# Four block products at once: the small matrix M computed from 64x64 tiles of the tensor engine

## The chip, the cores and the metric

The kernel runs on one core of a Trainium2 chip. The metric is the device time of one execution in microseconds (us). Every time quoted as a median comes from executions without the profiler; each profile is of one further execution, and its span (first to last instruction) is a little shorter than the device time of the same run: 260.0 us of span against 261.42 us for the kernel before. All profiles that an argument rests on are of fast runs; two runs of one experiment, and its profile, fell in a slower state, and that is said there. Some runs of the kernel before did too (five among those below: 266.08, 267.37, 266.89, 266.29 and 266.42 us); they count in its medians, but not in the ratios.

Engines are named as in the profile: PE is the tensor engine (TensorE), PEld its weight loads, DVE VectorE, ACT ScalarE, POOL GpSimd, SP SyncE. "SPq" is SyncE's sequencer issuing a transfer. The kernel's PSUM tensor `ps`, where the matmuls write, is laid out as eight banks of 512 columns, used singly or as four pairs. The granted clock is TensorE's clock in the profile, as a share of full speed. In the timelines a w2 tile is ten matmuls (five of 512 columns, five of 128) for 128 tokens, a w3 group is five 512-column matmuls whose result ACT copies out of PSUM as `h2T`, and an a-tile is the ten matmuls of attention for 128 tokens.

## The reference, cut to what matters

```python
# A: linear attention, 32 heads of 20 columns; S = 2048 tokens, D = 640
pq, pk = phi(q), phi(k)                            # phi = elu + 1
kv  = einsum("bhsd,bhse->bhde", pk, v)             # one 20x20 matrix per head
num = einsum("bhqd,bhde->bhqe", pq, kv)
o   = num / den
a   = o @ wo
# B: LayerNorm, w1, gelu, token shifts, w2, residual, LayerNorm, w3, gelu, w4
out = g * a + (1 - g) * b
```

The kernel never forms `o`. The 32 head matrices and `wo` are contracted into one 640x640 matrix M first, and attention for a tile of 128 tokens is then one product with the normalised queries, `pqnT`:

M = blockdiag(kv) · wo,  a-tile = (pq / den) · M.

`blockdiag(kv)` is cut into blocks of whole heads. `GT` is x^T·phi(k), so a block of kv comes from the value weights and `GT`; its off-diagonal heads are masked away on the way into `Lt`, which is the weight operand of the product with `wo`. M lies in SBUF as `M_sb`, five slots of 128 rows.

## The kernel before

Before the change a block is six heads, 120 columns: five blocks of 120, and one of 40 for the last two heads. Each block gets its own product of one 512-column and one 128-column matmul. Blocks of 120 leave rows 120 to 127 of each slot of `M_sb` free; the 40 rows of the last block go there. They are first written to `Mt` and then moved by five small transfers of eight rows.

```python
def kvt_group(h):                                   # kv blocks; 30 small matmuls over h = 0, 1
    ...
    for q_, r in enumerate(range(4) if h == 0 else range(4, 6)):
        n = min(R6, D - R6 * r)                     # R6 = 120
        for k in range(KD):                         # KD = 5
            mms.append((ps[:, b, R6 * q_:R6 * q_ + n], wvf[:, D * k + R6 * r:D * k + R6 * r + 128],
                        GT[:, k, R6 * r:R6 * r + n], ...))
...
def m_group(r):                                     # one block of M, recorded six times
    n = min(R6, D - R6 * r)
    kr = R6 if r < 5 else 128
    b = pair()
    mm_group(ps[:, b, 0:512], [(Lt[0:kr, r, :], wo_aug[0:kr, r, 0:512])])
    mm_group(ps[:, b + 1, 0:128], [(Lt[0:kr, r, :], wo_aug[0:kr, r, 512:D])])
    src = psf[0:n, 512 * b:512 * b + D]
    dst = M_sb[0:n, r, :] if r < 5 else Mt[0:n, :]
    activation(dst, src, ACTF.Copy)                 # ACT writes only rows 0 to 119 of M_sb

def m_tail():                                       # rows 120 to 127 of every slot
    for j in range(KD):
        sch.dma("sp", M_sb[R6:128, j, :], Mt[8 * j:8 * j + 8, :], "mt", group_total=KD)
...
for n, r in enumerate((5, 0, 1, 2, 3, 4)):          # the block that feeds Mt comes first
    IT.add("KVF", ("m", r), 0.0, lambda r=r: m_group(r),
           deps=[(("lt", 1), 1.0), (("w3", (1 + 3 * n) // KFF, (1 + 3 * n) % KFF), 0.0)])
IT.add("MT", ("mt",), 0.0, m_tail, deps=[(("m", 5), 1.5), (("t1", NT - 1), 0.0)])
...
def qt_tile(t):                                     # pqnT by transposing transfers, also on SyncE
    sch.dma("sp", pqnT[:, :, 128 * t:128 * (t + 1)], pq_tok[:, t, :], ..., transpose=True)

def a_tile(t):                                      # the first use of M
    ...
    mm_group(ps[:, b, 0:512], [(pqnT[:, j, tok], M_sb[:, j, 0:512]) for j in range(KD)])
    mm_group(ps[:, b + 1, 0:128], [(pqnT[:, j, tok], M_sb[:, j, 512:D]) for j in range(KD)])
```

## Time and profile before

Three runs before the prediction: 261.96, 266.08 and 263.4 us, median 263.4.

| what | value | read from |
|---|---|---|
| span | 260.0 us, granted clock 1.00 | cores view |
| PE busy | 254.7 us, 98% | page, part 1 |
| chain that ended last | 97% PE | page, part 4 |
| one M block, from its first matmul to the next ordinary one | 0.27 to 0.28 us in five of the six; behind the other one a matmul's record is missing | PE timeline |
| row moves into M | 5 issues in 3.49 us, from 115.97 | SP timeline |
| first use of M | 139.42 us, no wait | PE timeline |

The page of the kernel before, parts 1 and 4, is:

```profile
PE 254.7 (98%) x1671; PEld 135.9 (52%) x1703; DVE 148.9 (57%) x266; ACT 106.9 (41%) x215; POOL 96.8 (37%) x151
...
PE 97%; issue 1%; DVE 1%; POOL 0%; POOLq 0%
```

PE is the bottleneck nearly everywhere. A change helps only by taking time from PE, and hurts as soon as it makes PE wait.

The PE timeline of the kernel before follows. Here and in every timeline below the columns are: start in us, us from the first start to the last end, engine, source line, operation, output and inputs, their shapes, number of instructions, and in brackets the idle time before the group and what ended it.

```profile
92.34 1.52 PE L600 MATMUL ps<-w,hsT 128*128 128x512 bf16 x10
...
126.17 0.44 PE L600 MATMUL ps<-wo_aug,Lt 120*128 120x512 bf16 x2
126.45 1.24 PE L600 MATMUL ps<-xnT,w 128*128 128x512 bf16 x5
...
139.42 1.52 PE L600 MATMUL ps<-M_sb,pqnT 128*128 128x512 bf16 x10
```

The first line is w2 tile 4, after which the changed kernel does its first M products. An M block takes the slot from 126.17 to 126.45, since a matmul's recorded duration overlaps the next one's start. The last line is the first use of M. The distance from 92.34 to 139.42, 47.08 us, holds everything that the change does to M. I call it the **M stretch** and compare it in every run: it leaves out the start of the kernel, whose length varies between runs.

SyncE's issues in the kernel before, from the SP timeline:

```profile
115.97 3.49 SPq L285 DMA_DIRECT2D M_sb<-Mt  x5
119.51 6.66 SPq L281 DMA_TRANSPOSE xnT<-xn  x4
126.21 7.88 SPq L281 DMA_TRANSPOSE pqnT<-pq_tok  x6
```

The row moves are over by 119.5, and the first pqnT transpose is issued at 126.21, some 13 us before its use.

### The profile page before, as it was taken

To read this page: it belongs to the slowest core of one execution; us is meant where nothing else is said; L and a number is where in the kernel's file an instruction comes from. 1 tells how busy PE (TensorE), PEld (TensorE's weight loads), DVE (VectorE), ACT (ScalarE), POOL (GpSimd) and SP (SyncE) were. 2 spreads that over 40 slices of the span, in tenths; PEclk is the share of its full clock that TensorE was granted. 3 is DMA by queue.
4 is the path that set the end of the run, shared out by engine and by line. 5 is a ranking of instruction groups with operands and counts; after the bars stand their busy time and mean duration, and the time that the engine had idled before them with its cause. 6 is when DMAs were issued, how large, how long until landed. Compare 5 with 4: busy or idle time off the path is not lost.

```text
span 260.0 us, 4263 instructions
## 1 busy us (share of the span) xinstructions
PE 254.7 (98%) x1671; PEld 135.9 (52%) x1703; DVE 148.9 (57%) x266; ACT 106.9 (41%) x215; POOL 96.8 (37%) x151
## 2 busy tenths in 40 slices
PE   8999999999999999999999999999999999999996
PEld 4555555555555454555444545554455544455553
DVE  1597877899903799979994407992033410143333
ACT  1496777741355757674874240005500045100000
POOL 5013995859874017865854202230011100021001
PEclk9999999999999999999999999999999999999999
DMA  6855989642566894355565700232000020000311
GB/s 199 255 103 143 211 149 158 194 87 23 105 126 103 275 377 94 76 101 58 107 124 109 125 0 0 45 85 74 3 0 0 3 101 0 3 0 0 103 50 50
DMA packets 50691, 24.82 MB, mean 95 GB/s; under 512 B 42052, under 2 KB 49261, under 8 KB 50672
## 3 DMA queue, kind: packets, MB, share of 16 engines
q1 hardware_dynamic: 49280, 21.15, 35.8%
q0 software_dynamic: 1152, 3.28, 5.2%
q8 instruction: 13, 0.21, 0.3%
q10 hardware_dynamic: 240, 0.13, 0.2%
q14 instruction: 6, 0.05, 0.1%
HBM read 12.05 MB, written 2.62 MB: 56 GB/s over the span
## 4 chain that ended last, share of the span: by engine, by line
PE 97%; issue 1%; DVE 1%; POOL 0%; POOLq 0%
PE ps L600 61%; PE ps L1106 21%; PE ps L781 8%; PE ps L857 2%; PE ps L830 1%; PE ps L1020 1%; PE ps L1088 1%; DVE x_tok L639 1%; PE ps L858 1%; PE ps L611 1%; PE ps L934 1%; PE ps L1085 0%; POOL xn L659 0%; POOLq L1249 0%
## 5 line engine op out<-in xcount | busy, mean ns | idle before, releaser
L600 PE MATMUL ps<-xnT,w 128*128 128x512 bf16 x349 | 80.7, 379 | 0.5
L1106 PE MATMUL ps<-w,h2T 128*128 128x128 bf16 (+1 forms) x409 | 57.9, 298 | 0.7 <-issue 0.5
L656 ACT ACTIVATE h2T<-ps 128x512 bf16<-128x512 f32 x52 | 30.5, 600 | 65.6 <-PE ps L600 65.5
L600 PEld LDWEIGHTS ps<-xnT,w 128*128 128x128 bf16 x360 | 33.9, 98 | 36.9 <-issue 0.4
L639 DVE SCALAR_TENSOR_TENSOR x_tok<-ps,stg,abx 128x512 bf16<-128x512 f32 (+1 forms) x32 | 17.2, 551 | 61.6 <-PE ps L1106 61.6
L622 POOL TENSOR_SCALAR abx<-x_tok,stg 128x640 f32<-128x640 bf16 x16 | 14.8, 923 | 100.6 <-DVE x_tok L639 95.1
L1106 PEld LDWEIGHTS ps<-w,h2T 128*128 128x128 bf16 x416 | 32.4, 98 | 25.6 <-issue 1.1
L622 POOL TENSOR_SCALAR xn<-x_tok,st 128x640 bf16<-128x640 bf16 x32 | 36.8, 1155 | 15.4 <-DMA xnT<-xn 14.9
L656 ACT ACTIVATE Er<-ps 128x640 bf16<-128x640 f32 x32 | 22.4, 704 | 17.4 <-PE ps L600 8.5
L655 ACT ACTIVATE junk<-x_tok 128x640 bf16<-128x640 bf16 x32 | 23.6, 737 | 4.9 <-DVE x_tok L637 4.4
L656 ACT ACTIVATE hsT<-ps 128x512 bf16<-128x512 f32 (+1 forms) x32 | 18.9, 593 | 15.1 <-PE ps L600 12.7
L600 PE MATMUL ps<-w,hsT 128*128 128x512 bf16 (+1 forms) x159 | 23.8, 298 | 0.1
L600 PE MATMUL ps<-M_sb,pqnT 128*128 128x128 bf16 (+1 forms) x156 | 23.5, 297 | 0.3
L781 PE MATMUL ps<-pk_tok,x_tok 128*128 128x128 bf16 (+1 forms) x156 | 23.3, 297 | 0.2
L639 DVE SCALAR_TENSOR_TENSOR abx<-ps,stg,abx 128x640 f32<-128x640 f32 x16 | 14.1, 884 | 15.3 <-PE ps L600 15.3
L600 PE MATMUL ps<-wkg,xT 128*128 128x512 bf16 (+1 forms) x147 | 22.3, 298 | 0.2
L600 PEld LDWEIGHTS ps<-w,hsT 128*128 128x128 bf16 x160 | 13.3, 98 | 12.3
L600 PEld LDWEIGHTS ps<-M_sb,pqnT 128*128 128x128 bf16 x160 | 13.1, 98 | 10.4
L600 PE MATMUL ps<-wq,xT 128*128 128x512 bf16 (+1 forms) x119 | 18.2, 298 | 0.1
L622 DVE TENSOR_SCALAR Er<-Er 128x640 bf16<-128x640 bf16 x32 | 12.0, 376 | 9.1 <-ACT Er L656 8.8
L637 DVE SCALAR_TENSOR_TENSOR x_tok<-ps,x_tok 128x640 bf16<-128x640 f32 x16 | 13.1, 821 | 6.9 <-PE ps L600 6.0
L600 PEld LDWEIGHTS ps<-wkg,xT 128*128 128x128 bf16 x150 | 12.2, 97 | 9.0
(71 smaller groups left out, 230.0 us busy)
## 6 DMA issues: line engine op xcount, KB each, us to landing
w<-in_B_w_dram SPq DMA_DIRECT2D x1, 2160.0 KB, 8.2
w<-in_B_w_dram SPq DMA_DIRECT2D x1, 2080.0 KB, 13.7
x_tok<-in_A_x_dram SPq DMA_DIRECT2D x3, 640.0 KB, 5.7
out_dram<-x_tok SPq DMA_DIRECT2D x3, 640.0 KB, 3.5
w<-in_B_w_dram POOLq DMA_DIRECT2D x8, 160.0 KB, 4.8
wq<-in_A_wqkv_dram SPq DMA_DIRECT2D x5, 160.0 KB, 3.8
wkg<-in_A_wqkv_dram SPq DMA_DIRECT2D x5, 160.0 KB, 3.9
wv<-in_A_wqkv_dram POOLq DMA_DIRECT2D x1, 800.0 KB, 6.2
```

The source lines that it names most:

```text
L600: ins = e.matmul(out_ap, l, r, start=(i == 0), stop=(i == n - 1))
L611: ins = e.transpose(o, s_, ident[:])
L622: return engf(lambda e: e.tensor_scalar(out_ap, in_ap, s1, s2, op0, op1), rd, [out_ap], cost=cost)
L637: return dve(lambda e: e.scalar_tensor_tensor(out_ap, in0, scalar, in1, op0, op1, accum_out=accum), rd, [out_ap, accum], cost=cost + 70.0)
L639: return dve(lambda e: e.scalar_tensor_tensor(out_ap, in0, scalar, in1, op0, op1), rd, [out_ap], cost=cost)
L655: return act(lambda e: e.activation(out_ap, in_ap, func, bias=bias, scale=scale, accum_out=accum), rd, wr, cost=cost)
L656: return act(lambda e: e.activation(out_ap, in_ap, func, bias=bias, scale=scale), rd, wr, cost=cost)
L781: ins = e.matmul(o, l, r, start=(t0 + q_ == 0), stop=(t0 + q_ == NT - 1))
L830: ins = e.matmul(ps[:, b, 0:n], xn[:, 0, 0:128], xn[:, 0, 0:128].unsqueeze(1).to_broadcast([128, n // 128, 128]), start=True, stop=True)
L857: e.matmul(ps[:, b, 0:512], l, w[:, k, 0:512], start=(k == 0), stop=(k == KD - 1))
L858: return e.matmul(ps[:, b + 1, 0:n2], l, w[:, k, 512:512 + n2], start=(k == 0), stop=(k == KD - 1))
L1106: ins = e.matmul(o, l, r, start=False, stop=(i == KFF - 1), skip_group_check=(n0 > 0))
```

## The change

The intent: the six block products cost six passes through PE's array, one after the other, and most of each product meets zeros, since only the heads' own 20x20 matrices are kept. With blocks of 60 columns (three heads), the array can be addressed as four 64x64 tiles, and up to four block products run at once. Eleven blocks are then three passes instead of six: one of three products (the last of the eleven blocks has 40 columns), recorded after w2 tile 4 (`m_last`), and two of four (`m_first`), recorded after the eighth w3 group. I call each visit to 64x64 tiles an *excursion*.

For this the kernel holds kv blocks at partitions 0 and 64: ACT copies the value weights into pairs of 60-column blocks (`wv2`, 25 copies). It also takes six PSUM banks at once for `m_first`, where blocks from the two halves of the array are given different banks. And the layout of M changes: free rows are now 60 to 63 and 124 to 127 of each slot, so ten row moves of four rows replace five of eight. The evictions of `m_first` are copies over all 128 partitions, which overwrite the free rows, so the row moves have to follow `m_first`.

```diff
-R6 = 120
+B3 = 60
+    wv2 = ra.alias("wv2", [128, KD, 6, 128], BF16, ...)        # value weights in pairs of blocks
+    def wv_blocks(k):                                           # 5 ACT copies for each k, 25 in all
+        ...
+    def kvt_group(h):   # still 30 matmuls; weights from wv2, up to 160 columns
...
-    def m_group(r):
-        ...             # as above
+    def m_step(jobs, tails):
+        def fn(e):
+            ins = None
+            for step in jobs:
+                for n0, n1 in ((0, 512), (512, D)):
+                    for g, h, kr, bm, c, bs, q0 in step:
+                        o = ps[64 * c:64 * c + 64, bm, :] if n0 == 0 else ps[64 * c:64 * c + 64, bs, q0:q0 + 128]
+                        ins = e.matmul(o, Lt[64 * h:64 * h + kr, g, :], wo_aug[64 * h:64 * h + kr, g, n0:n1], start=True, stop=True, ...)
+            return ins
+        ...
+        for dst, bm, bs, q0, pr in tails:
+            activation(dst[pr, 0:512], ps[pr, bm, :], ACTF.Copy)
+            copy(dve, dst[pr, 512:D], ps[pr, bs, q0:q0 + 128])
+    def m_last():       # one step of three products, two bank pairs
+        ...
+    def m_first():      # two steps of four products, three bank pairs
+        ...             # tails: pr = slice(0, 128)
     def m_tail():
-        for j in range(KD):
-            sch.dma("sp", M_sb[R6:128, j, :], Mt[8 * j:8 * j + 8, :], "mt", group_total=KD)
+        for m in range(10):
+            p0 = 60 + 64 * (m % 2)
+            sch.dma("sp", M_sb[p0:p0 + 4, m // 2, :], Mt[4 * m:4 * m + 4, :], "mt", group_total=10)
...
-    for n, r in enumerate((5, 0, 1, 2, 3, 4)):
-        IT.add("KVF", ("m", r), 0.0, lambda r=r: m_group(r), deps=[...])
-    IT.add("MT", ("mt",), 0.0, m_tail, deps=[(("m", 5), 1.5), (("t1", NT - 1), 0.0)])
+    IT.add("KVF", ("m", 0), 0.0, m_last, deps=[(("lt", 1), 1.0), (("w1", 2, 2), 0.0)])
+    IT.add("KVF", ("m", 1), 0.0, m_first, deps=[(("lt", 1), 1.0), (("w3", 0, 3), 0.0)])
+    IT.add("MT", ("mt",), 0.0, m_tail, deps=[(("m", 1), 1.5), (("t1", NT - 1), 0.0)])
```

Cut from the diff: the masks, the loads of `wo_aug` in the new order, and the column order of the normalised queries, which follows M's rows.

More of the change, by code (lines that the diff above doesn't have):

```diff
@@ L467, in _build @@
     ident = pa.alloc("ident", [128, 128], BF16)
-    mask = pa.alloc("mask120", [128, 6, 20], BF16)
-    mask_t = pa.alloc("mask_t", [128, 6, 20], BF16)
+    mask = pa.alloc("mask60", [128, 3, 20], BF16)
+    mask_t = pa.alloc("mask_t", [128, 4, 3, 20], BF16)
     negh = pa.alloc("negh", [128, 4], F32)
@@ L483, in _build @@
     pq_tok = pa.alloc("pq_tok", [128, NT + 1, D], BF16)
-    Lt = pa.alloc("Lt", [128, 6, 128], BF16)
+    Lt = pa.alloc("Lt", [128, 6, 64], BF16)
     Mt = pa.alloc("Mt", [128, D], BF16)
@@ L495, in _build @@
     GT = ra.alias("GT", [128, KD, D], BF16, ra.last_addr, KD * S * 2)
+    wv2 = ra.alias("wv2", [128, KD, 6, 128], BF16, ra.last_addr + KD * D * 2, KD * (S - D) * 2)
     wkg = ra.alloc("wkg", [128, KD, NK], BF16)
@@ L709, in load_w2, with wo_rows @@
             sch.dma("pool", w2[32 * g_:32 * (g_ + 1), 4, :], B_w2[160 * g_ + 128:160 * (g_ + 1), :], "w2", group_total=8, deps=dp)
+    def wo_rows(h, e, ns):
+        v = A_wo[0:600, :].rearrange("(q p) d -> p q d", p=B3)
+        q0 = 2 * h + e
+        return v[:, q0:q0 + 4 * (ns - 1) + 1:4, :]
     def load_wvo():
@@ L713, in load_wvo @@
         sch.dma("pool", wv[:, :, :], A_wqkv[:, 2 * D:3 * D].rearrange("(k p) f -> p k f", p=128), "wv", deps=dp)
-        for r in range(6):
-            n = min(R6, D - R6 * r)
-            sch.dma("pool", wo_aug[0:n, r, :], A_wo[R6 * r:R6 * r + n, :], "wo", group_total=6, deps=dp)
+        for h in range(2):
+            for e in range(2):
+                ns = 3 - h
+                sch.dma("pool", wo_aug[64 * h:64 * h + B3, e:e + 2 * ns - 1:2, :],
+                        wo_rows(h, e, ns), "wo", group_total=5, deps=dp)
+        sch.dma("pool", wo_aug[64:104, 4, :], A_wo[600:D, :], "wo", group_total=5, deps=dp)
     memset(pool, xn[:, 0, 0:128], 1.0)
@@ L722, in _build @@
     memset(pool, negh[:], -0.5)
-    aselect(mask_t[0:120], ones_c[0:120, 0:120].rearrange("p (b d) -> p b d", b=6), [[-20, 6], [0, 20]], ALU.is_ge, 0, 1)
-    aselect(mask[0:120], mask_t[0:120], [[20, 6], [0, 20]], ALU.is_ge, 19, -1)
+    for h in range(2):
+        aselect(mask_t[:, 2 * h], ones_c[:, 0:B3].rearrange("p (b d) -> p b d", b=3), [[-20, 3], [0, 20]], ALU.is_ge, -64 * h, 1)
+        aselect(mask_t[:, 2 * h + 1], mask_t[:, 2 * h], [[20, 3], [0, 20]], ALU.is_ge, 19 + 64 * h, -1)
+    tt(pool, mask[:], mask_t[:, 1], mask_t[:, 3], ALU.add)
     memset(pool, Lt[:], 0.0)
     memset(pool, wvf[:, KD * D:], 0.0)
-    memset(pool, wo_aug[:, 5, :], 0.0)
     memset(pool, hsT[:, :, 0:4], 0.0)
@@ L916, in _build, with heads @@
         IT.add("GT", ("g", i), 1.36, lambda i=i: gt_step(i, NT - 5, NT), deps=[(("g0", NT - 1), 0.0)])
+    def wv_blocks(k):
+        def heads(lo, ns):
+            v = wvf[:, D * k + lo:D * k + lo + 240 * ns].rearrange("p (s c) -> p s c", s=ns)
+            return [v[:, :, 60 * e:60 * e + 64] for e in range(2)]
+        for h, ns in ((0, 3), (1, 2)):
+            for e, src in enumerate(heads(120 * h, ns)):
+                activation(wv2[:, k, e:e + 2 * ns - 1:2, 64 * h:64 * h + 64], src, ACTF.Copy)
+        src = wvf[:, D * k + 600:D * k + 664].unsqueeze(1).to_broadcast([128, 2, 64])
+        activation(wv2[:, k, 4:6, 64:128], src, ACTF.Copy)
+    for k in range(KD):
+        IT.add("WV", ("wv2", k), 0.0, lambda k=k: wv_blocks(k), deps=[(("k", NT - 1), 2.0), (("lwv",), 0.0), (("ga", 1), 0.0)])
     kv_bank = {}
+    KV0 = (0, 60, 240, 300, 480, 540)
     def kvt_group(h):
@@ L924, in kvt_group @@
         mms = []
-        for q_, r in enumerate(range(4) if h == 0 else range(4, 6)):
-            n = min(R6, D - R6 * r)
+        for q_, g in enumerate(range(4) if h == 0 else range(4, 6)):
+            c0 = KV0[g]
+            n1 = (B3, B3, B3, B3, 40, 0)[g]
             for k in range(KD):
-                mms.append((ps[:, b, R6 * q_:R6 * q_ + n], wvf[:, D * k + R6 * r:D * k + R6 * r + 128], GT[:, k, R6 * r:R6 * r + n],
-                            q_ == 0 and k == 0, k == KD - 1))
+                l = wv2[:, k, g, :]
+                if n1 == 60:
+                    r_ = GT[:, k, c0:c0 + 240].rearrange("p (a c) -> p a c", a=2)[:, :, 0:B3]
+                    o = ps[:, b, 120 * q_:120 * q_ + 120].rearrange("p (a c) -> p a c", a=2)
+                    mms.append((o, l, r_, q_ == 0 and k == 0, k == KD - 1))
+                elif n1:
+                    mms.append((ps[:, b, 120 * q_:120 * q_ + 160], l, GT[:, k, c0:c0 + 160], q_ == 0 and k == 0, k == KD - 1))
+                else:
+                    mms.append((ps[:, b, 160:160 + B3], l, GT[:, k, c0:c0 + B3], False, k == KD - 1))
         def fn(e):
@@ L935, in fn @@
             return ins
-        pe(fn, [wvf[:, :], GT[:, :, :]], [ps[:, b, 0:480], ps[:, b + 1, 0:1]], cost=len(mms) * 60.0)
+        pe(fn, [wv2[:, :, :, :], GT[:, :, :]], [ps[:, b, 0:480], ps[:, b + 1, 0:1]], cost=len(mms) * 60.0)
     def lt_evac(h):
         b = kv_bank[h]
-        for q_, r in enumerate(range(4) if h == 0 else range(4, 6)):
-            n = min(R6, D - R6 * r)
-            src = ps[0:n, b, R6 * q_:R6 * q_ + n].rearrange("p (h m i) -> p h m i", m=5, i=4)
-            msk = mask[0:n, 0:n // DH, :].rearrange("p h (m i) -> p h m i", i=4)
-            if r < 5:
-                dst = Lt[0:n, r, 0:n].rearrange("p (h m i) -> p h m i", m=5, i=4)
-            else:
-                dst = Lt[0:n, r, 0:n].rearrange("p (m h i) -> p h m i", m=5, i=4)
-            tt(dve, dst, src, msk, ALU.mult)
@@ L949, in lt_evac, with put @@
-        bank_hold.difference_update((b, b + 1))
-    def m_group(r):
-        n = min(R6, D - R6 * r)
-        kr = R6 if r < 5 else 128
-        b = pair()
-        mm_group(ps[:, b, 0:512], [(Lt[0:kr, r, :], wo_aug[0:kr, r, 0:512])])
-        mm_group(ps[:, b + 1, 0:128], [(Lt[0:kr, r, :], wo_aug[0:kr, r, 512:D])])
-        src = psf[0:n, 512 * b:512 * b + D]
-        dst = M_sb[0:n, r, :] if r < 5 else Mt[0:n, :]
-        activation(dst, src, ACTF.Copy)
+        def put(p0, n, q0, nq, c0, step, cols):
+            pr = slice(p0, p0 + n)
+            na = cols // DH
+            src = psf[pr, 512 * b + c0:512 * b + c0 + step * nq].rearrange("p (q c) -> p q c", q=nq)[:, :, 0:cols].rearrange("p q (a d) -> p q a d", d=DH)
+            dst = Lt[pr, q0:q0 + nq, 0:cols].rearrange("p q (a d) -> p q a d", d=DH)
+            tt(dve, dst, src, mask[pr, 0:na, :].unsqueeze(1).to_broadcast([n, nq, na, DH]), ALU.mult)
@@ new lines, in lt_evac @@
+        if h == 0:
+            put(0, B3, 0, 4, 0, 120, B3)
+            put(64, B3, 0, 4, 60, 120, B3)
+        else:
+            put(0, B3, 4, 2, 0, 160, B3)
+            put(64, 40, 4, 1, 120, 40, 40)
+        bank_hold.difference_update((b, b + 1))
+    def m_step(jobs, tails):
[5 more added lines that the diff above has]
+                        o = ps[64 * c:64 * c + 64, bm, :] if n0 == 0 else ps[64 * c:64 * c + 64, bs, q0:q0 + 128]
+                        ins = e.matmul(o, Lt[64 * h:64 * h + kr, g, :], wo_aug[64 * h:64 * h + kr, g, n0:n1], start=True, stop=True,
+                                       skip_group_check=True)
+            return ins
+        banks = sorted({x[3] for st_ in jobs for x in st_} | {x[5] for st_ in jobs for x in st_})
+        pe(fn, [Lt[:, :, :], wo_aug[:, :, :]], [ps[:, b, :] for b in banks], cost=len(jobs) * 300.0 + 190.0)
+        for dst, bm, bs, q0, pr in tails:
+            activation(dst[pr, 0:512], ps[pr, bm, :], ACTF.Copy)
+            copy(dve, dst[pr, 512:D], ps[pr, bs, q0:q0 + 128])
@@ new lines, in m_last @@
+    def m_last():
+        b, bt = pair(), pair()
+        m_step([[(4, 0, B3, b, 0, bt, 0), (5, 0, B3, b, 1, bt, 0), (4, 1, 40, b + 1, 0, bt + 1, 0)]],
+               [(Mt, b + 1, bt + 1, 0, slice(0, 40)), (M_sb[:, 4, :], b, bt, 0, slice(0, 128))])
+    def m_first():
+        pb = (pair(), pair())
+        bt = pair()
+        jobs, tails = [], []
+        for s_ in range(2):
+            jobs.append([(2 * s_ + c, h, B3, pb[s_] + h, c, bt + h, 128 * s_) for h in range(2) for c in range(2)])
+            tails += [(M_sb[:, 2 * s_ + h, :], pb[s_] + h, bt + h, 128 * s_, slice(0, 128)) for h in range(2)]
+        m_step(jobs, tails)
@@ L971, in _build @@
     for h in range(2):
-        IT.add("KVF", ("kvt", h), 0.0, lambda h=h: kvt_group(h), deps=[(("g", KD - 1), 1.0)])
+        IT.add("KVF", ("kvt", h), 0.0, lambda h=h: kvt_group(h), deps=[(("g", KD - 1), 1.0), (("wv2", KD - 1), 1.0)])
         IT.add("KVF", ("lt", h), 0.0, lambda h=h: lt_evac(h), deps=[(("kvt", h), 0.0)])
-    for n, r in enumerate((5, 0, 1, 2, 3, 4)):
-        IT.add("KVF", ("m", r), 0.0, lambda r=r: m_group(r), deps=[(("lt", 1), 1.0), (("w3", (1 + 3 * n) // KFF, (1 + 3 * n) % KFF), 0.0)])
-    IT.add("MT", ("mt",), 0.0, m_tail, deps=[(("m", 5), 1.5), (("t1", NT - 1), 0.0)])
+    IT.add("KVF", ("m", 0), 0.0, m_last, deps=[(("lt", 1), 1.0), (("w1", 2, 2), 0.0)])
+    IT.add("KVF", ("m", 1), 0.0, m_first, deps=[(("lt", 1), 1.0), (("w3", 0, 3), 0.0)])
+    IT.add("MT", ("mt",), 0.0, m_tail, deps=[(("m", 1), 1.5), (("t1", NT - 1), 0.0)])
     IT.add("ZB", ("zb",), 0.0, zb_group, deps=[(("z", NT - 1), 1.7), (("w2", 0), 0.0)])
@@ L1038, in qn_scale @@
         dve(lambda e: e.reciprocal(dnr[:, 1, sd, :], dnr[:, 0, sd, :]), [dnr[:, 0, sd, :]], [dnr[:, 1, sd, :]], cost=350.0)
-        blk = pq_tok[:, t, :].rearrange("p (j c) -> p j c", c=128)
-        main = (blk[:, :, 0:R6].rearrange("p j (a d) -> p j a d", d=DH),
-                pq_tok[:, t + 1, 0:5 * R6].rearrange("p (j a d) -> p j a d", a=6, d=DH),
-                dnr[:, 1, sd, 0:30].rearrange("p (j a) -> p j a", a=6).unsqueeze(3).to_broadcast([128, 5, 6, DH]), 850.0)
-        tail = (blk[:, :, R6:128].rearrange("p m (h i) -> p h m i", i=4),
-                pq_tok[:, t + 1, 5 * R6:D].rearrange("p (h m i) -> p h m i", h=2, i=4),
+        blk = pq_tok[:, t, :].rearrange("p (j c) -> p j c", c=64)
+        main = (blk[:, :, 0:B3].rearrange("p j (a d) -> p j a d", d=DH),
+                pq_tok[:, t + 1, 0:10 * B3].rearrange("p (j a d) -> p j a d", a=3, d=DH),
+                dnr[:, 1, sd, 0:30].rearrange("p (j a) -> p j a", a=3).unsqueeze(3).to_broadcast([128, 10, 3, DH]), 850.0)
+        tail = (blk[:, :, B3:64].rearrange("p (h m) i -> p h m i", h=2),
+                pq_tok[:, t + 1, 10 * B3:D].rearrange("p (h m i) -> p h m i", h=2, i=4),
                 dnr[:, 1, sd, 30:32].unsqueeze(2).unsqueeze(3).to_broadcast([128, 2, 5, 4]), 150.0)
@@ L1197, in _build @@
         c = t // 4
-        deps = [(("qt", t), 3.0), (("w4load",), 0.0), (("m", KD - 1), 1.0), (("mt",), 2.5)]
+        deps = [(("qt", t), 3.0), (("w4load",), 0.0), (("m", 1), 1.0), (("mt",), 2.5)]
         if t >= 4:
```

## The prediction

> **What bounds the kernel.** TensorE. The page's first part has PE busy 254.7 of 260.0 us (98%), the chain of waits is 97% PE, the granted clock is 1.00, and the waits view shows no PE wait over 0.5 us outside the start. Only PE time, or a new PE stall, can move the total. Back-to-back 512-column matmuls start 216 ns apart in the timeline, a 512+128 pair takes 0.27 us.
>
> **PE work removed.** Six M groups (one 512 and one 128 matmul each) stand alone in the timeline, 0.27 to 0.28 us each: 1.65 us. They become two excursions into 64x64 tiles: three products at once (ideal 0.27 us), then two steps of four (ideal 0.54 us). Excursions are not free. The kernel has three already, the half-row w4 matmuls: the first one's four concurrent pairs (ideal 0.54 us) take 0.81 us from its first matmul at 153.88 to the next ordinary one at 154.69, with weight loads not pulled ahead of it. [...] Estimate: 0.55 + 0.85 = 1.4 us. The kv products stay at 30 matmuls with slightly more columns: +0.1 us. Net PE work: -0.15 us.
>
> **Off PE.** ACT gets 25 small copies of value weights; from its copies (0.70 us for 640 columns, 0.60 for 512) about 0.3 us each, 7 to 8 us. They start after the first GT copy (ends 57.7), ACT sits idle 3.6 us twice before 67.0 and 2.1 before 71.1, and the value weights landed by about 53.3: they delay two GT copies but no bank is short. No cost. DVE loses two masking operations and gains five small copies (about 0.25 us each). The small row moves into M grow from 5 to 10 DMA issues at 0.62 us (6.2 us of SyncE) and now come after the second excursion, ahead of the first pqnT transposes; the first M use is some 13 us later, so I expect a margin of 1 to 2 us.
>
> **The new wait.** The second excursion needs three bank pairs at once, of four. It stands after the eighth w3 group, at about 125.4 us. There ACT is behind: before, it waited 2.1 us for DVE until 124.2, did the last square sum, then six h2T evictions in a burst, 0.5 us apart, from 124.95. At 125.4 five w3 banks are unread. Three pairs are free only after about three evictions, near 127. I expect PE to stall 1 to 2 us on ACT before the second excursion (none before the first, where ACT is idle), and nothing later to give it back.
>
> **Sum.** -0.15 + 1.4 = about +1.2 us, all on the critical path: 264.5 us, range 262.0 to 267.2 (the runs before spread over 4 us by themselves). Chances: faster over 2% 0.01, within 2% 0.95, slower over 2% 0.04.
>
> **What would show it.** The second excursion's first matmul waits for ACT h2T for 1 to 2 us; each excursion lasts 0.5 to 0.9 us until the next ordinary matmul; kv matmuls 1.5 us in all; W1 starts at 70 us as before; the first M use has no wait for DMA; PE busy nearly unchanged.
>
> **What would make it wrong.** If the banks come free in time, the result is 263.2, a wash. If weight loads of 64 columns serialize, the excursions cost up to 0.5 us more. If the 10 row moves or the late transposes hold the first M use, up to 3 us more. If ACT's small copies cost far more than 0.3 us, W1's first groups stall. A DVE pushed later by the copies would delay the last square sum, and with it everything in that burst.

Its sum came to about +1.2 us and 264.5 us: the two excursions stand in it with 0.55 + 0.85 = 1.4 us, an estimate from their ideals of 0.27 and 0.54 with about 0.27 us more for each, the 0.81 less 0.54 us read in the profile before.

## More of the kernel before

`IT.add(stream, name, duration, function, deps)` is read by a list scheduler at build time. It chooses the order in which the pieces are recorded, so a changed dependency moves instructions on every engine's queue.

SyncE's queue holds, in this part of the kernel, three kinds of transfer: the row moves, the transposes of `xnT` (the second LayerNorm's output, which feeds the w3 groups) and the transposes of `pqnT`.

## The result, and the profile after

| kernel | median us | range | runs |
|---|---|---|---|
| before | 262.38 | 261.91 to 266.08 | 6 |
| after | 264.12 | 263.51 to 264.22 | 6 |

The ratio is 1.0059, with an interval of 1.0034 to 1.0083. Ratios in this document are those of the record, from fast runs alone and against the kernel before in the same rounds, so they are not quite the ratio of the medians quoted. The interval is clear of 1, so the kernel is a little slower. A later repeat (`after_again`, below) gave 264.22 us and 1.0076. The output was correct. The time lies inside the predicted range, 0.4 us under the predicted 264.5.

Parts 1 and 4 of the page of the kernel after:

```profile
PE 257.4 (98%) x1713; PEld 135.6 (52%) x1713; DVE 150.4 (57%) x270; ACT 111.8 (43%) x240; POOL 96.1 (37%) x152
...
PE 94%; ACT 1%; SPq 1%; DVE 1%; DMA 1%; issue 0%; POOL 0%; POOLq 0%
```

The chain has fallen from 97% PE to 94%, and ACT, SyncE's queue and a DMA have come into it. (PE's busy sum rose by 2.7 us, but this cannot be read as added matmul time: the start of this run was slower, as said below, and products that run at once and records that the trace lacks both change what the sum counts.) Two waits of PE are new. The waits view of the kernel after has them; its columns are engine and line, the releaser, then us in total, how often, longest us:

```profile
PE ps L601 <- DMA pqnT<-pq_tok: 1.7, 1, 1.7
...
PE ps L994 <- ACT h2T L657: 0.4, 1, 0.4
```

The PE timeline of the kernel after shows where they stand:

```profile
93.11 1.52 PE L601 MATMUL ps<-w,hsT 128*128 128x512 bf16 x10
94.56 0.46 PE L994 MATMUL ps<-wo_aug,Lt 60*64 60x512 bf16 x6
94.96 1.25 PE L601 MATMUL ps<-xnT,w 128*128 128x512 bf16 x5
...
126.71 0.74 PE L994 MATMUL ps<-wo_aug,Lt 60*64 60x512 bf16 x16 [0.45 <-ACT h2T L657]
127.38 13.12 PE L601 MATMUL ps<-xnT,w 128*128 128x512 bf16 x60
142.21 1.53 PE L601 MATMUL ps<-M_sb,pqnT 128*128 128x512 bf16 x10 [1.70 <-DMA pqnT<-pq_tok]
```

The M stretch is now 93.11 to 142.21, 49.10 us: 2.02 longer than before. From the first use of M to the end both kernels take the same, 120.6 us (the span less the start of the a-tile). So the change is paid in the M stretch.

The rest of the 2.8 us between the two profiled spans is 0.77 us that the kernel after is late at its w2 tile 4 (93.11 against 92.34). Some 0.68 us of that is there already at 13 us, ahead of any PE work that was changed: the first two 512-column matmuls behind 5.1 us took 0.58 and 0.63 us in this run, where the kernel before has 0.38 and 0.39. (The other 0.09 is that of the kv products, below.) The cause was not shown: the windows view has a granted clock of 1.00 there in both. I take it to belong to the run and not to the change: among the experiments below one with the changed start reached w2 tile 4 at 92.69 (rows_early), and one with the old start at 92.97 (before_rows_late2). It was not tested further.

The wait for pqnT has its cause on SyncE. The SP timeline of the kernel after:

```profile
131.19 6.98 SPq L285 DMA_DIRECT2D M_sb<-Mt  x10
138.23 1.24 SPq L281 DMA_TRANSPOSE xnT<-xn  x1
139.51 7.89 SPq L281 DMA_TRANSPOSE pqnT<-pq_tok  x6
```

The first pqnT transpose is issued at 139.51, where before it was at 126.21. Ten row moves and one xnT transpose stand in front of it. The chain of waits of the kernel after runs through these from 135.75 on (its columns are start us, us, and what). Further back the view leaves SyncE for an ACT eviction of `h2T`, which I take for a wrong guess of its releaser: that eviction ended at 135.75, when the move that it is said to release had been running since 135.31.

```profile
135.93 0.58 SPq L285
...
138.23 1.24 SPq L281
...
139.51 2.65 DMA pqnT<-pq_tok
```

And the row moves themselves start only at 131.19, though `m_first` was over at 127.4. The evictions of `m_first`, which they have to follow, were done at 129.56. Two xnT transposes are ahead of them in the queue, and these waited for GpSimd, which normalises the rows that they transpose. The POOL timelines of the kernel before and of the kernel after, at the point where the last statistics (`st`) arrive:

```profile
124.05 0.88 POOL L622 TENSOR_SCALAR xn<-x_tok,st 128x640 bf16<-128x640 bf16 x1 [2.94 <-DMA xnT<-xn]
124.91 1.56 POOL L622 TENSOR_SCALAR st<-st 128x4 f32<-128x4 f32 x2
```

```profile
124.05 0.20 POOL L623 TENSOR_SCALAR st<-st 128x4 f32<-128x4 f32 x1
...
127.55 3.17 POOL L623 TENSOR_SCALAR xn<-x_tok,st 128x640 bf16<-128x640 bf16 x3
```

The scheduler recorded the pieces in another order: before, one normalisation came ahead of the statistics; after, it stands behind them and runs from 127.55. The xnT transposes of this normalisation and of the next could not be issued until 128.46 and 129.90.

### The profile page after: what moved, and what is told of

Read it like the earlier page. It is cut to its first block, busy times and chain, and to the rows that moved or that the text cites. A ratio compares the mean times of both kernels' runs of the same rounds, so it can differ in the third digit from the quotient of the medians.

```text
span 262.8 us, 4353 instructions
## 1 busy us (share of the span) xinstructions
PE 257.4 (98%) x1713; PEld 135.6 (52%) x1713; DVE 150.4 (57%) x270; ACT 111.8 (43%) x240; POOL 96.1 (37%) x152
## 4 chain that ended last, share of the span: by engine, by line
PE 94%; ACT 1%; SPq 1%; DVE 1%; DMA 1%; issue 0%; POOL 0%; POOLq 0%
PE ps L601 57%; PE ps L1163 21%; PE ps L791 8%; PE ps L867 2%; PE ps L840 1%; DMA pqnT<-pq_tok 1%; ACT h2T L657 1%; PE ps L1077 1%; PE ps L1145 1%; SPq L285 1%; DVE x_tok L640 1%; PE ps L612 1%; PE ps L966 1%; PE ps L868 1%; SPq L281 0%; PE ps L994 0%
## 5 line engine op out<-in xcount | busy, mean ns | idle before, releaser
L601 PE MATMUL ps<-xnT,w 128*128 128x512 bf16 x360 | 81.6, 379 | 0.0
L1163 PE MATMUL ps<-w,h2T 128*128 128x512 bf16 (+1 forms) x416 | 58.8, 299 | 0.0
L623 POOL TENSOR_SCALAR xn<-x_tok,st 128x640 bf16<-128x640 bf16 x32 | 37.7, 1184 | 7.0 <-DMA xnT<-xn 6.6
L601 PE MATMUL ps<-M_sb,pqnT 128*128 128x512 bf16 (+1 forms) x160 | 24.4, 299 | 1.7 <-DMA pqnT<-pq_tok 1.7
L791 PE MATMUL ps<-pk_tok,x_tok 128*128 128x512 bf16 (+1 forms) x160 | 23.9, 299 | 0.0
L791 PEld LDWEIGHTS ps<-pk_tok,x_tok 128*128 128x128 bf16 x160 | 12.4, 98 | 8.4
```

What stands on the lines that cost most here:

```text
L601: ins = e.matmul(out_ap, l, r, start=(i == 0), stop=(i == n - 1))
L623: return engf(lambda e: e.tensor_scalar(out_ap, in_ap, s1, s2, op0, op1), rd, [out_ap], cost=cost)
L791: ins = e.matmul(o, l, r, start=(t0 + q_ == 0), stop=(t0 + q_ == NT - 1))
L1163: ins = e.matmul(o, l, r, start=False, stop=(i == KFF - 1), skip_group_check=(n0 > 0))
```

## The experiments

The theory (T): nearly all of the 2 us is SyncE's queue. Ten row moves that must follow `m_first` stand ahead of the first pqnT transpose, and their *issue* time delays it past the moment at which PE needs it. The rival (R): the loss is in PE's own visit to the tiles, in what it takes to enter and leave them, the loads and the 0.45 us for banks, and the row moves only take slack. A third possibility (B): the wait for banks delays everything behind it, so curing it cures the rest.

The runs were made on three chips, those of each group with their own runs of the kernel before. The M stretch is read from each one's PE timeline.

| run | group | median us (range, runs) | ratio to before | M stretch | wait for banks | wait at first use of M |
|---|---|---|---|---|---|---|
| before | – | 262.38 (261.91–266.08, 6) | 1 | 47.08 | 0 | 0 |
| after | – | 264.12 (263.51–264.22, 6) | 1.0059 | 49.10 | 0.45 | 1.70 |
| moves5 | 1 | 262.60 (262.01–263.18, 4) | 1.0005 | 47.24 | 0.46 | 0 |
| moves15 | 1 | 269.14 (268.66–269.86, 4) | 1.0264 | 52.21 | 0.46 | 4.81 |
| rows_split | 1 | 262.35 (262.06–262.76, 4) | 0.9997 | 47.24 | 0.46 | 0 |
| m1_late | 1 | 274.30 (273.62–274.91, 4) | 1.0451 | 57.21 | 0 | 10.34 |
| rows_early_late | 2 | 261.79 (261.30–262.65, 6) | 0.9969 | 46.71 | 0 | 0 |
| rows_early | 2 | 262.10 (261.98–262.29, 4) | 0.9976 | 47.17 | 0.39 | 0 |
| steps_twice | 2 | 262.21 (261.99–262.91, 4) | 0.9986 | 47.25 | 0 | 0 |
| before_rows_late | 2 | 269.77 (264.93–271.46, 4) | 1.0153 | slow profile | – | – |
| after_again | 3 | 264.22 (263.94–264.50, 5) | 1.0076 | 49.12 | 0.45 | 1.72 |
| rows_early_late2 | 3 | 261.55 (261.37–261.81, 5) | 0.9977 | about 46.7 | 0 | 0 |
| before_rows_late2 | 3 | 266.51 (265.35–267.14, 4) | 1.0159 | 50.28 | 0 | 3.03 |

In rows_early_late2 the record of the first matmul of the a-tile is missing, so its M stretch is worked out from the second. The kernel before had medians of 262.06 (7 runs), 263.03 (11) and 262.27 (9) in the three groups. In group 2 slow runs lift that median in part; without them it is 262.72.

### moves5: half of the row moves

```diff
-        for m in range(10):
+        for m in range(0, 10, 2):
             p0 = 60 + 64 * (m % 2)
-            sch.dma("sp", ..., "mt", group_total=10)
+            sch.dma("sp", ..., "mt", group_total=5)
```

This leaves the rows 124 to 127 of M unset, so its result is wrong. (The comparison with the reference still passed: by the code those rows hold zeros, copied from PSUM, and their share of the output must be below its tolerance. A pass is no proof that a small part of M is right.)

> Changed kernel with only 5 of the 10 row moves issued (wrong result on purpose: half of the moved rows of M stay unset). Theory A, the SyncE queue: in the changed kernel the first M use (a-tile 0) stands 1.9 us late because 10 row moves of 0.70 us each sit ahead of the first pqnT transpose; with 5 moves (3.5 us) that transpose lands near 138.7, before PE asks at 140.3, so the wait goes from 1.7 to 0 and the time falls by 1.9 us, to about 262.2. Theory B, the 64x64 excursions and the wait for banks make up the loss: the time stays at 264.1. Under both the 0.45 us wait for banks before the second excursion stays.

The wait at the first use of M went from 1.70 us to nothing, the M stretch from 49.10 to 47.24, and the time to 262.60 us, as the kernel before. The SP timeline of moves5:

```profile
131.51 3.43 SPq L285 DMA_DIRECT2D M_sb<-Mt  x5
...
136.24 8.25 SPq L281 DMA_TRANSPOSE pqnT<-pq_tok  x6
```

The moves still start late, at 131.5, but five of them take 3.43 us in place of 6.98, and pqnT is issued at 136.24, in time. The wait for banks is unchanged (0.46 us), so it is not what holds the first use of M: B falls, and R explains at most what is left.

### moves15: five more moves behind the ten

```diff
+        for m in range(5):
+            sch.dma("sp", Mt[64 + 4 * m:68 + 4 * m, :], Mt[4 * m:4 * m + 4, :], "mt2", group_total=5)
```

> Changed kernel with 5 more row moves of the same size, into rows of a scratch tile that nobody reads, issued right after the 10 (right result). Theory A: 5 x 0.70 = 3.5 us more in front of the first pqnT transpose, and as this wait is already exposed all of it shows: the first M use waits 5.2 us, time 267.6. Theory B: no change, 264.1.

Nothing reads what these five write; they only take SyncE's time. They took 3.06 us there, as the SP timeline of moves15 shows:

```profile
138.09 3.06 SPq L285 DMA_DIRECT2D Mt<-Mt  x5
```

The M stretch grew by 3.11 us over that of the kernel after. Once the queue is the last to arrive, its issue time is paid one for one. The PE timeline of moves15:

```profile
145.17 2.85 PE L601 MATMUL ps<-M_sb,pqnT 128*128 128x512 bf16 x10 [4.81 <-DMA pqnT<-pq_tok]
147.81 1.53 PE L601 MATMUL ps<-xnT,w 128*128 128x512 bf16 x5
```

The time of 269.14 us is more than 3 us above after. One reason stands in these lines: after a wait of 4.81 us the next a-tile took 2.64 us to the following group, where it takes 1.36 in the kernel before. The mean granted clock was 0.994 in this run and 0.987 in the three others. By the windows view the clock was 1.00 up to 145 us, 0.50 from 145 to 146, 0.70 from 146 to 150, and 1.00 again behind that: it was lower just behind the wait, and PE paid again. So only the M stretch, which ends before the part at the lower clock, is used for the size.

### rows_split: half of the moves issued by another engine

```diff
-            sch.dma("sp", ..., "mt", group_total=10)
+            sch.dma("pool" if m % 2 else "sp", ..., "mt%d" % (m % 2), group_total=5)
```

> Changed kernel, every second row move issued by GpSimd instead of SyncE (right result). Theory A: as with 5 moves, wait at the first M use 0 and time 262.2, if GpSimd's five moves land before 140.3 us (they should be issued from about 130.7, some 0.6 us each, and land 2 to 5 us later, so near 139). Theory B: no change, 264.1.

The PE timeline of rows_split, at its w2 tile 4 and its first use of M, and its SP timeline:

```profile
93.61 1.52 PE L601 MATMUL ps<-w,hsT 128*128 128x512 bf16 x10
...
140.85 1.52 PE L601 MATMUL ps<-M_sb,pqnT 128*128 128x512 bf16 x10
```

```profile
131.70 3.43 SPq L285 DMA_DIRECT2D M_sb<-Mt  x5
...
136.44 8.24 SPq L281 DMA_TRANSPOSE pqnT<-pq_tok  x6
```

All ten moves are made, the result is right, and the transfers carry the same bytes. Only the sequencer that issues half of them is another. The wait at the first use of M is gone, the M stretch is 47.24 us exactly as in moves5, and the time is that of the kernel before (0.9997). So the cost is not the moving of the rows but the issuing on SyncE.

How long GpSimd's own five issues took and when they landed is not given here. My figures for them (0.6 us each, 2 to 5 us to landing) were estimates: for its 16 loads of `w` in the kernel after, the source view has 0.75 us an issue in the median (0.51 to 1.14), and the page, part 6, 4.1 us to landing.

One issue on SyncE, 0.58 us as a rule, is a third of the 1.78 us from the start of the last move's issue in m1_late (148.75) to PE's start on its rows (150.53). But the issues stand one behind the other: ten of them held SyncE for 6.98 us, for 51 KB of rows (four rows of 640 two-byte numbers, ten times), and issuing five elsewhere took 1.86 us off the M stretch.

### m1_late: the second excursion three groups later

```diff
-    IT.add("KVF", ("m", 1), 0.0, m_first, deps=[(("lt", 1), 1.0), (("w3", 0, 3), 0.0)])
+    IT.add("KVF", ("m", 1), 0.0, m_first, deps=[(("lt", 1), 1.0), (("w3", 0, 8), 0.0)])
```

> Changed kernel, the second excursion allowed only from the ninth w3 group on; it is then recorded after the eleventh, where ACT has caught up, and the row moves come after the first six pqnT transposes in SyncE's queue. Theory A: the wait for banks (0.45 us) goes to 0 but saves nothing, as the first M use now waits for the row moves themselves: six transposes end near 140.3, ten moves at 0.70 us end near 147.3, landing about 149: the first M use comes some 7 us later than in the changed kernel and the time is about 271. Theory B, the wait for banks is the loss: 263.7.

The wait for banks disappeared (the excursion started at 129.64 with no idle time before it), and the kernel became 10 us slower. The waits view of m1_late has one large line, and the SP timeline shows why:

```profile
PE ps L601 <- DMA M_sb<-Mt: 10.3, 1, 10.3
```

```profile
134.33 7.89 SPq L281 DMA_TRANSPOSE pqnT<-pq_tok  x6
142.34 6.98 SPq L285 DMA_DIRECT2D M_sb<-Mt  x10
```

The scheduler now put the row moves behind six pqnT transposes. PE waits for the last moved row in place of the first transpose. I had expected 271 us: I had placed the moves 2 us earlier in the queue, and had not reckoned with the clock (0.975 to 0.981 over the whole runs, which hold a wait of 10.34 us). The direction was right. A cure for the 0.45 us that leaves the row moves waiting for `m_first` is no cure here.

### rows_early_late and rows_early: the moves taken off the critical path

The evictions of `m_first` are split, so that they no longer write the free rows. The row moves then depend only on `m_last`, some 30 us earlier. In rows_early_late the second excursion also stands two groups later than in the kernel after.

```diff
         for dst, bm, bs, q0, pr in tails:
-            activation(dst[pr, 0:512], ps[pr, bm, :], ACTF.Copy)
-            copy(dve, dst[pr, 512:D], ps[pr, bs, q0:q0 + 128])
+            for p_ in (pr,) if pr.stop < 128 else (slice(0, B3), slice(64, 64 + B3)):
+                activation(dst[p_, 0:512], ps[p_, bm, :], ACTF.Copy)
+                copy(dve, dst[p_, 512:D], ps[p_, bs, q0:q0 + 128])
-    IT.add("KVF", ("m", 1), 0.0, m_first, deps=[(("lt", 1), 1.0), (("w3", 0, 3), 0.0)])
-    IT.add("MT", ("mt",), 0.0, m_tail, deps=[(("m", 1), 1.5), (("t1", NT - 1), 0.0)])
+    IT.add("KVF", ("m", 1), 0.0, m_first, deps=[(("lt", 1), 1.0), (("w3", 0, 8), 0.0)])   # rows_early: this line as in the kernel after
+    IT.add("MT", ("mt",), 0.0, m_tail, deps=[(("m", 0), 1.5), (("t1", NT - 1), 0.0)])
```

> Changed kernel with both waits designed away (right result): M is copied out in the two row blocks 0-59 and 64-123, so that the moved rows are not overwritten and the ten moves can go right after the first excursion, where SyncE has been idle (near 97 us); and the second excursion is recorded only after the tenth w3 group, where ACT has read the banks. Theory A: wait for banks 0 (was 0.45), wait at the first M use 0 (was 1.7 to 1.9); left are the PE work saved in M (0.33 us, from the traces: 1.66 before, 0.50 and 0.83 after) less 0.1 for the kv products, so 0.2 us below the kernel before: ratio 0.999. If ratio is above 1.003, something of the loss is still unexplained, such as a hidden cost of the excursions or of the regrouping.

> As rows_early_late, but the second excursion where the recording scheduler puts it, now after the seventh w3 group, in the middle of ACT's backlog. Theory A: no wait at the first M use, but a wait for banks of 1.0 to 1.5 us at the second excursion, all of it in the time: ratio 1.003 to 1.005. If the bank wait costs nothing by itself, the ratio equals that of rows_early_late.

In rows_early_late neither wait is left. Its PE timeline:

```profile
94.11 1.52 PE L601 MATMUL ps<-w,hsT 128*128 128x512 bf16 x10
...
129.35 0.74 PE L994 MATMUL ps<-wo_aug,Lt 60*64 60x512 bf16 x16
130.02 10.96 PE L601 MATMUL ps<-xnT,w 128*128 128x512 bf16 x50
140.82 1.52 PE L601 MATMUL ps<-M_sb,pqnT 128*128 128x512 bf16 x10
```

The M stretch is 46.71 us, 0.37 shorter than in the kernel before. This is what the 64x64 tiles are worth to PE when nothing waits. The median of 261.79 us is below that of the kernel before, and the ratio 0.9969 lies just clear of 1 (0.9940 to 0.9998).

In rows_early the wait for banks was 0.39 us where I had expected 1.0 to 1.5. That expectation was a miss, and its cause stays open. The M stretch is 47.17, 0.46 longer than in rows_early_late, which is what placing the excursion where ACT is behind costs.

### steps_twice: what one step of four products costs

On top of rows_early_late, the two steps of the second excursion are done twice, in the same banks with the same values.

```diff
-            for step in jobs:
+            for step in (jobs if len(jobs) == 1 else jobs + jobs):
```

> As rows_early_late, with the two steps of the second excursion issued twice over (same results written again, right result). If the four products of a step really run at once, a step costs one product, 0.27 us: the excursion grows from about 0.83 us to 1.4 us, and the time by 0.55 us. If they run one after the other or are held by weight loads, it grows by 1 to 2 us.

The PE timeline of steps_twice:

```profile
128.32 1.28 PE L994 MATMUL ps<-wo_aug,Lt 60*64 60x512 bf16 x32
129.53 10.96 PE L601 MATMUL ps<-xnT,w 128*128 128x512 bf16 x50
```

The excursion takes 1.21 us from its first matmul to the next ordinary one, against 0.67 in rows_early_late, and the M stretch grew by 0.54. Two further steps of four products cost 0.54 us, so a step costs 0.27 us: just what a single 512-column and 128-column pair costs in the kernel before. The four products do run at once. So the loads of 64-column weights do not hold the products up here: that fear of the prediction ("up to 0.5 us more", an estimate) and of R is refuted.

What is left of the excursion's time is fixed: 0.67 − 0.54 = 0.13 us at its exit, and about 0.10 from the end of the last ordinary matmul's slot (129.25, one start-to-start distance of 0.216 after that matmul's start) to its first one, 0.77 us in all. The first excursion has the same: from the end of the slot before it, 94.47, to 94.96 is 0.49, of which one step is 0.27. So entering and leaving costs about 0.22 to 0.23 us, if the first steps cost what the two added ones did.

### before_rows_late and before_rows_late2: the same queue without any tiles

If T is right, late row moves must hurt the kernel *before* too, where nothing uses 64x64 tiles.

```diff
-        for j in range(KD):
-            sch.dma("sp", M_sb[R6:128, j, :], Mt[8 * j:8 * j + 8, :], "mt", group_total=KD)
+        for m in range(2 * KD):
+            p0 = R6 + 4 * (m % 2)
+            sch.dma("sp", M_sb[p0:p0 + 4, m // 2, :], Mt[4 * m:4 * m + 4, :], "mt", group_total=2 * KD)
# and dependencies: the moves after xnT transpose 12; the first pqnT transpose after the moves;
# xnT transpose 14 after the first pqnT transpose
```

> The kernel before, without any 64x64 tile: its 5 row moves cut into 10 of 4 rows each, issued after the fourteenth xnT transpose of the second norm and ahead of the first pqnT transpose (right result). Theory A: transposes done near 133.6, ten moves of 0.70 us to 140.6, first pqnT landing near 143.2, while PE asks at 139.4: a wait of about 3.8 us for DMA at the first M use, time about 265.9, although nothing else is changed. Theory B (64x64 excursions are the loss): no change, 262.1.

The first try was no use: its profile and two of its four runs fell in the slow state, with a stall of 3.5 us for an input transpose at 42 to 45 us. The fast runs' ratio of 1.0153 had the expected sign. The same kernel was run again in group 3.

> The kernel of before_rows_late once more, as its profile fell in the slow state. Expected in a fast profile: first M use waits about 2.8 us for the first pqnT transpose, the matmuls after that wait run at a lower clock for some 2 us, ratio of fast runs near 1.015.

It gave 266.51 us, ratio 1.0159 (1.0132 to 1.0186). Its SP timeline and its PE timeline:

```profile
134.12 6.37 SPq L285 DMA_DIRECT2D M_sb<-Mt  x10
140.53 8.21 SPq L281 DMA_TRANSPOSE pqnT<-pq_tok  x6
```

```profile
143.25 1.53 PE L600 MATMUL ps<-M_sb,pqnT 128*128 128x512 bf16 x10 [3.03 <-DMA pqnT<-pq_tok]
```

The M stretch is 50.28 us, 3.20 longer than in the kernel before, with a wait of 3.03 us (I had expected 3.8). The tiles are not needed for the loss. Of its four runs two kept a clock of 1.0 (265.35 and 266.08 us), and two had 0.994 (266.94 and 267.14). The profiled one kept 1.00 in every stretch after its wait, so the lower clock that I had expected behind it was a miss (the slow profile of before_rows_late had 0.68 from 146 to 150 us). Whether the wait lowered the clock in the two others is not shown: they were not traced, and the kernel before has runs at 0.994 too (266.42 us in this group) without such a wait.

### after_again and rows_early_late2: the two compared directly

> The changed kernel once more, so that it stands beside the repaired version on the same chip. Expected: 1.005 to 1.008 of the kernel before, as at first; wait for banks 0.45 us and wait at the first M use 1.7 us again in the trace. From the first matmul of w2 tile 4 to the first matmul of a-tile 0, which leaves the unsteady start out: 49.1 us, as in the first trace (47.1 in the kernel before).

> The repaired version once more (the kernel of rows_early_late unchanged). Expected: 46.7 us from w2 tile 4 to a-tile 0, 0.37 us less than in the kernel before; ratio to the kernel before 0.997 to 1.000; about 2.2 us below the changed kernel of the same rounds. If it isn't below the kernel before in this interval of the trace, the gain of the first run was luck.

On one chip in the same rounds: the kernel after 264.22 us, the kernel with early row moves and a later second excursion 261.55, the kernel before 262.27. The ratio of the second to the kernel before is 0.9977 (0.9962 to 0.9991). It beats both kernels: the kernel after by 2.67 us between the medians, the kernel before by 0.7. Its SP timeline shows the moves where they harm nothing:

```profile
95.52 6.36 SPq L285 DMA_DIRECT2D M_sb<-Mt  x10
...
129.22 8.24 SPq L281 DMA_TRANSPOSE pqnT<-pq_tok  x6
```

Of the 0.7 us gained on the kernel before, 0.37 is shown in the M stretch. The rest is not shown: the interval of the ratio reaches from 0.2 to 1.0 us and so holds 0.37 alone, and the time up to w2 tile 4 varies between runs by more than that (92.34 to 94.11 us among the profiles here).

## Why the prediction was right, point by point

The predicted time was right, 264.5 against 264.12 and 264.22. The sum behind it was right in part only: two of its terms were wrong in opposite directions, and it started from a base that was 1 us too high (263.4, the median of three runs of which one, 266.08, was slow; later 262.4). Going from the kernel before to the kernel after by way of two experiments divides the 2.02 us. That the parts add up is so by construction; their sizes are measured:

| step | M stretch | difference | predicted |
|---|---|---|---|
| before to rows_early_late: PE's work, no waits | 47.08 to 46.71 | −0.37 | −0.25 (1.65 to 1.4) |
| to rows_split: wait for banks | 46.71 to 47.24 | +0.53 | +1 to +2 |
| to after: row moves ahead of pqnT | 47.24 to 49.10 | +1.86 | 0 |
| sum | | +2.02 | about +1.2 with the kv products' +0.1 |

The difference in the second row holds the 0.46 us of the wait itself; the third is the wait of 1.70 us at the first use of M, and a little more before it is recorded (PE could have gone on at 140.33, pqnT landed at 142.16).

- **"What bounds the kernel. TensorE": right.** In moves15 3.06 us of added issues lengthened the M stretch by 3.11.
- **"PE work removed": right in direction and nearly in size.** 1.65 us became 0.49 + 0.77 = 1.26 us in rows_early_late (0.83 for the second excursion in the kernel after, without its wait), where 1.4 was predicted. But the reading behind the 0.27 us for an excursion (0.81 less 0.54) was faulty. It rested on the half-row excursion from 153.81 to 154.69 in the PE timeline of the kernel before, whose next group shows an idle time that only "issue" ended, and 25 matmuls where the program has 26: the record of the first is missing. Of the four excursions of this kind the last, from 241.65, is whole:

```profile
153.81 0.39 PE L1088 MATMUL ps<-w,h2h 64*128 64x512 bf16 x2
...
154.69 3.48 PE L1106 MATMUL ps<-w,h2T 128*128 128x512 bf16 x25 [0.16 <-issue]
...
241.65 0.39 PE L1088 MATMUL ps<-w,h2h 64*128 64x512 bf16 x2
...
242.30 10.77 PE L1106 MATMUL ps<-w,h2T 128*128 128x512 bf16 x77
```

  The whole one takes 0.65 us, 0.11 above the ideal 0.54, not 0.27. That the estimate came out near the truth is because it had also left out the 0.09 to 0.10 us before the first matmul: 0.27 was too much for the exit (0.13 in the 64x64 excursion), and near the 0.22 to 0.23 of exit and entry together. That is luck. (Weight loads were not pulled ahead, as the prediction says: by the PEld timeline the first load of these two excursions starts with its first matmul, at 153.81 and 241.65, where the load for the first use of M starts at 139.21, 0.21 us before its matmul.) The kv products cost 0.09 us more (4.77 us against 4.68 from the first of them to the next stage), as predicted.
- **"Off PE … No cost": right, with the sizes off.** ACT's 25 copies took 5.61 us, not 7 to 8, as its timeline shows, DVE's small copies of M took 0.27 to 0.29 us each (source view; expected 0.25), and nothing in the stage behind them was delayed.

```profile
58.25 5.61 ACT L657 ACTIVATE wv<-wv 128x192 bf16<-128x192 bf16 x25
```

- **"The new wait": right in cause, wrong in size.** PE did wait for ACT's h2T eviction before the second excursion, but 0.45 us and not 1 to 2. I had timed ACT from the profile before, where its burst of evictions starts at 124.95, and had PE arrive at 125.4. In the kernel after the burst starts at 124.62 and PE arrives at 126.1:

```profile
124.62 2.52 ACT L657 ACTIVATE h2T<-ps 128x512 bf16<-128x512 f32 x5
127.50 2.06 ACT L657 ACTIVATE M_sb<-ps 128x512 bf16<-128x512 f32 x4 [0.35 <-PE ps L994]
```

  The whole run is 0.77 us late at w2 tile 4. Counted from there, PE arrived as predicted (33.0 us behind it; predicted 33.1), and it was ACT's burst that began 1.1 us earlier (31.5 us behind it in place of 32.6). The predicted wait was the difference of the two. Why ACT was earlier was not tested. The kernel gives blocks from the two halves of the array different banks, and as written takes six of eight at once; no run here shows whether fewer would do. rows_early_late, which asks for the six two groups later, does not wait.
- **"The small row move … I expect a margin of 1 to 2 us": wrong, and this is the step that failed.** In place of the margin there was a wait of 1.70 us. The count of ten and the unit cost were nearly right (0.70 us each in place of 0.62). What was wrong was where the ten stand in the queue. The prediction gives no start for them; my working had them start at the end of the second excursion, about 128.7, and pqnT land at about 138.9. The evictions that they have to follow were done only at 129.56, and they started at 131.19, behind two xnT transposes which waited for GpSimd; one more xnT transpose of 1.24 us followed them, and pqnT landed at 142.16. Of these 3.3 us, 2.5 are the late start and 0.8 the costlier moves (6.98 us in place of 6.2). "If the 10 row moves or the late transposes hold the first M use, up to 3 us more" was among the risks named; the sum left it out. moves5, rows_split and rows_early each remove this wait by another way, moves15 lengthens it one for one, and before_rows_late2 makes it without any tiles.
- **"W1 starts at 70 us as before": right** (70.49 against 69.81; the difference is that of the run's start, told above). **"The first M use has no wait for DMA": wrong**, as above.

So the right total owes something to luck: a wait for banks that was predicted about 1 us too large, and a base 1 us too high, stood in for a wait of 1.9 us that the sum did not hold.

## What to carry to other kernels

A change that saves PE time can cost more through its bookkeeping: here 0.4 us of saved matmul time was paid for with 1.9 us because ten small moves on one engine's queue came between the last product and the transposes behind them. For every transfer that a change makes later or more numerous, write down what stands before it and behind it in the queue of the engine that issues it, and count issue time per transfer, not bytes (0.577 us for a move of 5 KB and 0.625 for one of 10 KB here, in the median); then take the dependency away (here by not overwriting the free rows) or split the issuing. When timing such an engine, use the order of the *changed* kernel: a margin that is a difference of two times read from the old profile does not survive a reordering.

## What the traces show of the hardware

- Issues add up on one queue. For one move the issue is 0.58 us of 1.78 (m1_late), but ten moves held SyncE for 6.98 us in the kernel after, and issuing five of them elsewhere took 1.86 us off the M stretch (rows_split).
- A move of four rows (5 KB) took SyncE 0.58 to 0.73 us in the kernel after (10 in 6.98 us; 10 in 6.35 in rows_early_late), a move of eight rows (10 KB) 0.62 to 0.78 in the kernel before (5 in 3.49 us), and a transposing transfer mostly 1.2 to 1.3 us in both. For the moves the cost goes nearly with their number: twice the bytes took 8% longer in the median (0.625 us against 0.577).
- One visit to 64x64 tiles cost 0.22 to 0.23 us beyond its steps, about 0.10 at its entry and 0.13 at its exit, all causes together (rows_early_late and steps_twice).
- A wait of PE may or may not cost clock behind it. In before_rows_late2 one of 3.03 us left it at 1.00, and in moves15 one of 4.81 us was followed by 0.70 from 146 to 150 us. In the profile of before_rows_late PE waited 2.74 us at the first use of M, the clock was 0.68 from 146 to 150 us and the a-tile took 2.64 us in place of 1.36; but that was a slow run, so it does not show that the wait was the cause.
